# Attention with a feed-forward layer: identity made on chip, first pair transposed ahead of the bias table product, one AV in two parts, alpha early, two feed-forward tiles first

## Chip, cores, metric

One core of one Trainium2 chip. The metric is the device time of one execution in microseconds (us). The kernel before takes 390.5 us (median of three runs, 390.46 to 390.96). Each execution also comes with the span from first to last instruction (about 1.7 us shorter than the time) and with the mean granted clock of the tensor engine. All moments below are us from the start of the span. PE is the tensor engine, ACT the scalar, DVE the vector engine, POOL is GpSimd.

## The reference

```python
# q, k, v: 8 x 8 x 576 x 64; bias_table: 32 x 8; w_in: 512 x 2048; w_out: 2048 x 512; alpha: 2048
scores = np.matmul(q, k.transpose(0, 1, 3, 2)) / np.sqrt(D)
scores = scores + bias.transpose(2, 0, 1)[None]      # bias depends on |i - j| alone
attn = softmax(scores)                               # ... max, exp, sum written out
attn_out = np.matmul(attn, v)
x = attn_out.transpose(0, 2, 1, 3).reshape(4608, 512)
h = x @ w_in
g = h + np.sin(alpha * h) ** 2 / (alpha + 1e-9)
return (g @ w_out).astype(np.float32)
```

## The kernel before

The kernel emits a start-up by hand and leaves the rest to a small list scheduler, which is part of the kernel's own Python: each task has a priority, an earliest planned moment (`nb`), buffers and dependencies, and the scheduler emits tasks in the order in which its model of the engines would start them. So a moved number moves the instruction order on every engine. Names: `natb`, `nat1` are q and k as loaded; `turn`/`plan_tr` transposes them on PE with the identity `id_sb`; `u` is exp(scores), multiplied on DVE by exp(bias) (`m2r`, `mhr`), made on chip from a table product; AV multiplies `u` by `v`, whose extra column of ones gives the sum; `am`, `ca`, `cb` are single PSUM banks, `sc` are the large ones. Heads go in pairs, four pairs per batch.

```python
T_START = 7.0
T_PAIR = ((7.0, 8.5), (10.5, 13.0), (10.5, 13.0))   # earliest transposes of pairs 1 to 3
T_W = 30.0
T_WO = (56.0, 59.0, 62.0, 65.0)                     # earliest use of the quarters of w_out
WARM0 = 6
WARM1 = 1
# ... start-up
    nc.sync.dma_start(out=id_sb, in_=idm.ap())      # identity from memory
    # ... loads of q, k, v
    nc.vector.tensor_tensor(out=tabN, in0=tabN, in1=tabL, op=ALU.subtract)
    nc.scalar.activation(out=tabE, in_=tabN, func=AF.Exp)
    warm(WARM0)
    eps_ = bank("moE")                              # bias table product, bank cb
    nc.tensor.matmul(out=eps_[0:H, 0:EW], lhsT=tabE, rhs=phi_sb, start=True, stop=True)
    warm(WARM1)
    nc.scalar.activation(out=e_sb, in_=eps_[0:H, 0:EW], func=AF.Copy)
    nc.scalar.dma_start(out=e_dram.ap(), in_=e_sb)
    cast0(0, nc.vector)
    cast0(1, P_)
    # ... POOL: bias rows, V casts, w_in loads, loads of the next batches
    stage_kq(2)
    load_w_out16()                                  # w_out in four quarters
    # ... plan_tr: transposes of pair 0 are tasks like any other
# ... plan_alpha
        m = plan.add({"PE": 0.1}, mm, [], 5000, nb=20.0, new=[b])
        return plan.add({"DVE": 0.4}, cp, [m], 5000, use=[b])
# ... plan_av: per 128 rows one matmul with vh and eight with v, all after every part of u
        for i, qc in enumerate(QC[w]):
            # ... 1 + 2 * 4 matmuls
            prev = [plan.add({"PE": 0.31}, mm, us + prev, base + AV_PRI + i, ...)]
# ... plan_moe_in: first feed-forward block; three quarters of each sum can start early
            if b == 0 and f < 4:
                m = plan.add({"PE": 3 * t_pe(512)}, lambda e, mm=mm: mm(e, range(3)), xs012,
                             pri - 100, nb=T_W, after=qk_last[:], new=[hb])
                m = plan.add({"PE": t_pe(512)}, lambda e, mm=mm: mm(e, range(3, 4)), xs + [m],
                             pri, use=[hb])
```

The softmax here doesn't subtract the row's maximum and nothing guards it: scores larger than these inputs give would overflow.

## Time and profile before

| stage of the kernel before | from - to | length | what fills it |
|---|---|---|---|
| start-up | 0 - 10.30 | 10.30 | loads, bias table, first transposes |
| 24 exponentials of batch 0 | 10.30 - 32.86 | 22.56 | ACT, with gaps |
| handover to the feed-forward block | 32.86 - 38.38 | 5.52 | DVE, PE, ACT in turn |
| first block of sines | 38.38 - 54.96 | 16.58 | ACT |
| exponentials of batches 1 and 2 | 54.96 - 95.72 | 40.76 | ACT, then PE |
| the rest | 95.72 - 388.7 | 293.0 | PE |

The borders are marks: first exponential, end of the last exponential of batch 0, first sine, second load of ACT's tables ("table load 2"; the load for the sines is the one before), and table load 3 at 95.72. Of the page, the first part (busy time, share of the span, instructions) and the fourth (the chain that ended last, by engine) of the kernel before:

```profile
PE 374.4 (96%) x3381; PEld 186.8 (48%) x3381; DVE 264.7 (68%) x588; ACT 319.1 (82%) x449; POOL 82.5 (21%) x96
PE 90%; ACT 5%; DVE 1%; issue 1%; DMA 1%; ACTq 0%; DVEq 0%
```

PE has something in flight for 96% of the time, so what a change of the first 55 us can win is the moment at which PE becomes dense. One thing to know about this page: its row of tenths for the clock shows 9 from the first slice on, while the matmul spacing of the warm-ups (0.426 us for 512 columns, 0.215 later) says that the array runs at half rate until its recorded release, at 22.43. That stretch the row does not show.

### The profile page before, as it was taken

The page shows a single profiled execution, that of the slowest core. Times are in us where ns is not written, and L with a number is a line of the kernel's source. Part 1 is how long each engine was busy: PE and PEld are TensorE (multiplying, and loading weights), DVE is VectorE, ACT ScalarE, POOL GpSimd, SP SyncE. Part 2 cuts the span into 40 slices and gives each one's busy share as a digit, 9 for nine tenths or more (in the row PEclk, how much of TensorE's full clock was granted, in tenths as well). Part 3 has the DMA queues.
Part 4 walks back from the last instruction along what each step waited for, and adds up shares of the span by engine and source line. Part 5 has one row for each costly group of instructions (what it writes and reads, how often), then busy time and mean ns, then how long its engine had stood idle before and what let it go on. Part 6 is the DMA issues. An engine that isn't in the chain of part 4 may idle for free.

```text
span 388.7 us, 8498 instructions
## 1 busy us (share of the span) xinstructions
PE 374.4 (96%) x3381; PEld 186.8 (48%) x3381; DVE 264.7 (68%) x588; ACT 319.1 (82%) x449; POOL 82.5 (21%) x96
## 2 busy tenths in 40 slices
PE   5999989999999999999999999999999999999995
PEld 2466434465545544555355435643554444444442
DVE  3776976776886798669767977697669628439100
ACT  2876999999999999999999999999999629539211
POOL 5673935072530081006200400000000000000000
PEclk9999999999999999999999999999999999999999
DMA  9999999999999999969991928210120020020112
GB/s 173 205 201 218 169 186 168 153 163 140 146 162 145 179 138 139 167 90 86 153 160 47 74 31 211 64 27 29 33 68 18 29 81 1 29 81 2 65 70 81
DMA packets 151207, 42.58 MB, mean 110 GB/s; under 512 B 140344, under 2 KB 145552, under 8 KB 151168
## 3 DMA queue, kind: packets, MB, share of 16 engines
q0 software_dynamic: 89872, 19.04, 59.5%
q1 hardware_dynamic: 61072, 22.95, 32.7%
q8 instruction: 26, 0.43, 0.5%
q14 instruction: 13, 0.11, 0.1%
q10 hardware_dynamic: 224, 0.05, 0.1%
HBM read 37.76 MB, written 16.52 MB: 140 GB/s over the span
## 4 chain that ended last, share of the span: by engine, by line
PE 90%; ACT 5%; DVE 1%; issue 1%; DMA 1%; ACTq 0%; DVEq 0%
PE sc L451 43%; PE am L451 37%; PE ca L451 4%; ACT u L719 4%; PE cb L451 4%; DMA tabL<-in_bias_table_dram 1%; PE cb L560 1%; PE am L560 1%; DVE kT L540 0%; ACT L953 0%; ACT outs L538 0%; ACT sq L886 0%; DVE xp L799 0%; DVE tabN L505 0%; ACT s L879 0%
## 5 line engine op out<-in xcount | busy, mean ns | idle before, releaser
L719 ACT ACTIVATE u<-sc 128x1024 f16<-128x1024 f32 (+1 forms) x192 | 155.7, 896 | 9.0 <-PE sc L451 7.0
L451 PE MATMUL sc<-xT,w_in 128*128 128x512 f16 x576 | 133.0, 379 | 0.2 <-DVE g L893 0.2
L893 DVE SCALAR_TENSOR_TENSOR g<-sq,inv_a,sc 128x512 f16<-128x512 f16 x144 | 103.8, 746 | 25.9 <-PE am L451 21.4
L451 PE MATMUL am<-w_out,g 128*128 128x512 f16 x448 | 117.3, 382 | 0.7 <-ACT outs L538 0.7
L879 ACT ACTIVATE s<-sc,alphaT 128x512 f16<-128x512 f32 x144 | 92.5, 679 | 7.0 <-PE sc L451 6.2
L744 DVE TENSOR_TENSOR u<-u,m2r 128x512 f16<-128x512 f16 (+2 forms) x160 | 67.8, 440 | 29.2 <-ACT u L719 27.0
L451 PEld LDWEIGHTS <-g 128*128 128x128 f16 x576 | 53.6, 98 | 67.4 <-issue 14.7
L451 PEld LDWEIGHTS <-w_in 128*128 128x128 f16 x576 | 54.6, 98 | 62.8 <-issue 0.3
L451 PEld LDWEIGHTS <-u 128*128 128x128 f16 x1440 | 55.9, 98 | 17.1 <-issue 4.5
L451 PE MATMUL am<-v,u 128*128 128x65 f16 x1216 | 53.4, 194 | 0.0
L451 PE MATMUL sc<-qT,kT 64*128 64x64 f16 (+1 forms) x512 | 48.2, 296 | 2.8 <-ACT u L719 1.0
L886 ACT ACTIVATE sq<-s 128x512 f16<-128x512 f16 x75 | 46.6, 630 | 2.3 <-DVE g L893 0.5
L397 POOL DMA_DIRECT2D v<-in_v_dram x24 | 21.2, 897 | 108.3 <-PE am L451 107.1
L451 PE MATMUL am<-vh,u 128*128 128x130 f16 x152 | 33.8, 222 | 0.7 <-DVE xp L799 0.6
L888 DVE TENSOR_TENSOR sq<-s 128x512 f16<-128x512 f16 x69 | 28.9, 420 | 6.6 <-ACT s L879 6.3
L799 DVE TENSOR_TENSOR xp<-am,rd 128x384 f16<-128x384 f32 (+1 forms) x56 | 27.5, 491 | 2.3 <-DVE rd L798 0.3
L451 PEld LDWEIGHTS <-kT 64*128 64x128 f16 x512 | 13.8, 96 | 30.1 <-issue 26.8
L798 DVE RECIPROCAL rd<-am 128x6 f32<-128x6 f32 (+1 forms) x60 | 11.3, 188 | 19.4 <-PE am L451 19.0
L538 ACT ACTIVATE outs<-am 128x512 f32<-128x512 f32 x7 | 4.2, 597 | 18.5 <-PE am L451 18.5
L953 ACT ACT_TABLE_LOAD x13 | 16.7, 1283 | 0.2
L540 DVE COPY outs<-am 128x512 f32<-128x512 f32 x21 | 14.4, 687 | 3.6 <-PE am L451 3.0
L378 POOL DMA_DIRECT2D staged_q<-in_q_dram x6 | 14.4, 2396 | 7.4 <-DMA staged_q<-in_q_dram 5.4
(87 smaller groups left out, 169.0 us busy)
## 6 DMA issues: line engine op xcount, KB each, us to landing
out_dram<-outs SPq DMA_DIRECT2D x36, 256.0 KB, 2.0
staged_k<-in_k_dram POOLq DMA_DIRECT2D x6, 576.0 KB, 15.9
staged_q<-in_q_dram POOLq DMA_DIRECT2D x6, 576.0 KB, 19.9
v<-in_v_dram POOLq DMA_DIRECT2D x24, 128.0 KB, 9.3
w_in<-in_moe_w_in_dram POOLq DMA_DIRECT2D x4, 512.0 KB, 8.1
w_out<-in_moe_w_out_dram POOLq DMA_DIRECT2D x4, 512.0 KB, 18.1
xT<-xp SPq DMA_TRANSPOSE x72, 4.4
w_out<-in_v_dram SPq DMA_DIRECT2D x4, 256.0 KB, 8.5
```

What stands on the lines that cost most here:

```text
L378: nc.gpsimd.dma_start(out=dst.ap()[t].rearrange("s (h d) -> s h d", h=H), in_=src[t].rearrange("h s d -> s h d"),)
L397: nc.gpsimd.dma_start(out=vs[t % 2][:, c, :, 0:D], in_=vp[128 * c : 128 * c + 128],)
L451: nc.tensor.matmul(out=out, lhsT=lhsT, rhs=rhs, start=start, stop=stop)
L540: k_of(e).tensor_copy(out=o, in_=i)
L719: nc.scalar.activation(out=o, in_=x, func=AF.Exp, scale=0.125)
L744: nc.vector.tensor_tensor(out=io, in0=io, in1=m2[:, 2 * p : 2 * p + 2, x0 : x0 + hi - lo], op=ALU.mult,)
L799: nc.vector.tensor_tensor(out=y.rearrange("p c (z d) -> p c z d", z=2), in0=a[:, :, :, 0:D], in1=r.unsqueeze(3).to_broadcast([128, nq, 2, ...
L879: nc.scalar.activation(out=s16.v, in_=h.v, func=AF.Sin, scale=alphaT[:, f : f + 1])
L886: nc.scalar.activation(out=sq.v, in_=s16.v, func=AF.Square)
L888: k_of(e).tensor_tensor(out=sq.v, in0=s16.v, in1=s16.v, op=ALU.mult)
L893: nc.vector.scalar_tensor_tensor(out=gcell[b].v[:, f, :], in0=sq.v, scalar=inv_a[:, f : f + 1], in1=h.v, op0=ALU.mult, op1=ALU.add,)
L953: nc.scalar.preload_act_table_set(name)
```

## The change

Its intent is a shorter start: no load of the identity; transposes of the first pair before the bias table product instead of behind it; the last pair's AV of the first batch in two parts, so that most of it need not wait for the last multiplications; alpha's transpose and reciprocal moved from the handover to the beginning. With it come new planned moments, a new priority for two of the first four feed-forward tiles, and a shorter list of dependencies for one AV task of each pair in the first batch (not shown below). Cut to its core:

```diff
-T_PAIR = ((7.0, 8.5), (10.5, 13.0), (10.5, 13.0))
+T_FREE = {"PE": 7.0, "ACT": 7.5, "DVE": 7.85}
+T_QT0 = 7.85
+T_PAIR = ((6.6, 7.3), (10.5, 13.0), (10.5, 13.0))
-WARM1 = 1
-    nc.sync.dma_start(out=id_sb, in_=idm.ap())
+    P_.memset(id_sb, 1.0)
+    P_.affine_select(out=id_sb, in_=id_sb, pattern=[[-1, 128]], compare_op=ALU.is_equal,
+                     fill=0.0, base=0, channel_multiplier=1)
+    cast0(0, nc.vector)
+    cast0(1, P_)
+    def turn0(kq):  # six transposes into one bank, copy by DVE
+        ...
+    turn0(0)
-    eps_ = bank("moE")
+    eps_ = new_ps("am0")
     nc.tensor.matmul(out=eps_[0:H, 0:EW], lhsT=tabE, rhs=phi_sb, start=True, stop=True)
-    warm(WARM1)
     nc.scalar.activation(out=e_sb, in_=eps_[0:H, 0:EW], func=AF.Copy)
     nc.scalar.dma_start(out=e_dram.ap(), in_=e_sb)
-    cast0(0, nc.vector)
-    cast0(1, P_)
+    turn0(1)
 # plan_alpha
-        m = plan.add({"PE": 0.1}, mm, [], 5000, nb=20.0, new=[b])
-        return plan.add({"DVE": 0.4}, cp, [m], 5000, use=[b])
+        m = plan.add({"PE": 0.1}, mm, [], -50, nb=8.0, new=[b])
+        return plan.add({"DVE": 0.4}, cp, [m], -50, use=[b])
 # plan_av
+        split = t == 0 and p == NP - 1 and w == 0
+        if split:
+            def part(e):  # the 18 matmuls on the first three parts of u
+                ...
+            prev = [plan.add({"PE": 0.62}, part, us[:3], base + AV_PRI, nb=T_V[t], new=[ab], use=[ub])]
 # plan_moe_in
-                             pri - 100, nb=T_W, after=qk_last[:], new=[hb])
+                             pri - (100 if f < 2 else 1), nb=T_W, after=qk_last[:], new=[hb])
```

More of the change, by code (lines that the diff above doesn't have):

```diff
@@ L109, in run @@
     def run(self, t0):
-        free = {e: t0 for e in ("PE", "ACT", "DVE", "POOL", "DMA", "SP")}
+        free = {e: T_FREE.get(e, t0) for e in ("PE", "ACT", "DVE", "POOL", "DMA", "SP")}
         todo = list(self.tasks)
@@ L254 @@
     phi_h = nc.inline_tensor(phi_np, "phi_const")
-    idm = nc.inline_tensor(np.eye(128, dtype=np.float16), "ident")
     idf = nc.inline_tensor(np.eye(NF, dtype=np.float32), "identf")
@@ L493 @@
         load_nat(nat1[:, kq, 0:2], 2, 4, src[0], P_)
+    P_.memset(id_sb, 1.0)
+    P_.affine_select(
+        out=id_sb, in_=id_sb, pattern=[[-1, 128]], compare_op=ALU.is_equal, fill=0.0, base=0,
+        channel_multiplier=1,
+    )
     vp = v[0].rearrange("h s d -> s h d")
@@ L507 @@
     warm(WARM0)
-    eps_ = bank("moE")
+    cast0(0, nc.vector)
+    cast0(1, P_)
+    def turn0(kq):
+        c = bank("moE").bitcast(F16)
+        for i in range(SI):
+            nc.tensor.transpose(
+                out=c[:, i * SN : i * SN + SN], in_=natb[:, kq, i], identity=id_sb[0:SN, 0:SN]
+            )
+        nc.vector.tensor_copy(
+            out=(qTs if kq else kTs)[0][:, 0, :].rearrange("d (p i) -> d p i", i=SI),
+            in_=c[:, 0:S].rearrange("d (i p) -> d p i", i=SI),
+        )
+    turn0(0)
+    eps_ = new_ps("am0")
     nc.tensor.matmul(out=eps_[0:H, 0:EW], lhsT=tabE, rhs=phi_sb, start=True, stop=True)
-    warm(WARM1)
     nc.scalar.activation(out=e_sb, in_=eps_[0:H, 0:EW], func=AF.Copy)
     nc.scalar.dma_start(out=e_dram.ap(), in_=e_sb)
-    cast0(0, nc.vector)
-    cast0(1, P_)
+    turn0(1)
     clear(P_, 1)
@@ L547, in plan_tr, with tail @@
         far = kq == 0 and (t == 1 or p > FAR)
+        def tail(e):
+            for z in range(2):
+                r = slice(64 * z, 64 * z + 64)
+                nc.vector.tensor_copy(
+                    out=kts[t][r, p, r], in_=kTs[t][r, p, 512:S]
+                )
+        if t == 0 and p == 0:
+            x = Task({}, None, [], 0)
+            x.end = T_QT0
+            return [x], [x] if kq else [plan.add({"DVE": 0.25}, tail, [x], pri + 30)]
         def mm(e):
@@ L552, in mm @@
                 x = i * SN
-                if t == 0 and p == 0:
-                    nc.tensor.transpose(
-                        out=c.v[:, x : x + SN], in_=natb[:, kq, i], identity=id_sb[0:SN, 0:SN]
-                    )
-                    continue
                 for z in range(2):
@@ L570, in cp @@
             copy_on(e, dst.rearrange("d (p i) -> d p i", i=SI), pin)
-        m = plan.add({"PE": 0.4 if t == 0 and p == 0 else 0.5}, mm, deps, pri, nb, new=[b])
+        m = plan.add({"PE": 0.5}, mm, deps, pri, nb, new=[b])
         eng = {"DVE": 0.75, "ACT": 0.72}
         if t == 0:
-            eng = {"ACT": 0.72} if p == 0 and kq else {"DVE": eng["DVE"]}
+            eng = {"DVE": eng["DVE"]}
         x = plan.add(eng, cp, [m], pri, use=[b])
@@ L593, in plan_tr @@
             return [x], []
-        def tail(e):
-            for z in range(2):
-                r = slice(64 * z, 64 * z + 64)
-                nc.vector.tensor_copy(
-                    out=kts[t][r, p, r], in_=kTs[t][r, p, 512:S]
-                )
         return [x], [plan.add({"DVE": 0.25}, tail, [x], pri + 30)]
@@ L770, in plan_av @@
         prev = []
+        split = t == 0 and p == NP - 1 and w == 0
+        if split:
+            def part(e):
+                av.v = bank(ab.tag)
+                for i, qc in enumerate(QC[w]):
+                    for z in range(2):
+                        for c in range(3):
+                            x0 = 2 * VC * i + VC * z
+                            full(av.v[:, x0 : x0 + VC], u.v[:, 4 * z + c, qc : qc + 128],
+                                 vs[t % 2][:, c, 2 * p + z, :], (i, z, c) == (0, 0, 0), False)
+            prev = [plan.add({"PE": 0.62}, part, us[:3], base + AV_PRI, nb=T_V[t], new=[ab],
+                             use=[ub])]
         for i, qc in enumerate(QC[w]):
             def mm(e, i=i, qc=qc):
-                if i == 0:
+                if i == 0 and not split:
                     av.v = bank(ab.tag)
@@ L777, in mm @@
                 full(av.v[:, x0 : x0 + 2 * VC], u.v[:, 8, qc : qc + 128], vhs[t % 2][:, p, :],
-                     True, False)
+                     not split, False)
                 for z in range(2):
-                    for c in range(4):
+                    for c in range(3 if split else 0, 4):
                         full(av.v[:, x0 + VC * z : x0 + VC * z + VC],
                              u.v[:, 4 * z + c, qc : qc + 128], vs[t % 2][:, c, 2 * p + z, :],
-                             False, z == 1 and c == 3)
-            prev = [plan.add({"PE": 0.31}, mm, us + prev, base + AV_PRI + i,
-                             nb=T_V[t] if t < 2 else 0.0, new=[ab] if i == 0 else [],
-                             use=[ub] if i == 0 else [ub, ab])]
+                             False, z == 1 and c == 3 and (not split or i == nq - 1))
+            needs = us
+            if t == 0 and w == 1 and i == 0:
+                needs = [done[(0, c)] for c in range(4)] + [done[(1, 4)]]
+            prev = [plan.add({"PE": 0.12 if split else 0.31}, mm, needs + prev,
+                             base + AV_PRI + i, nb=T_V[t] if t < 2 else 0.0,
+                             new=[ab] if i == 0 and not split else [],
+                             use=[ub] if i == 0 and not split else [ub, ab])]
             avs.setdefault(t, []).extend(prev)
```

## The prediction

> **What bounds the kernel now.** I read the page first: PE is busy for 96% of the span and 90% of the chain that ended last. So the span is PE work plus whatever keeps PE from it, and I asked next where PE is not dense. The table of busy time by stage (each row: stretch and length in us, then busy us with instruction counts of PE, weight loads, DVE, ACT, POOL, then clock, DMA share, GB/s) answers that:
>
> ```profile
> 0.00:10.30 10.30, 6.25 (x36) 2.61 (x36) 4.40 (x14) 2.73 (x4) 5.74 (x16) 1.00 0.97 178
> 10.30:22.40 12.10, 11.84 (x125) 6.15 (x123) 8.08 (x16) 10.20 (x12) 9.49 (x15) 1.00 1.00 199
> 22.40:32.87 10.47, 9.37 (x160) 6.57 (x158) 9.46 (x32) 9.61 (x12) 5.35 (x8) 1.00 1.10 203
> 32.87:38.38 5.51, 5.09 (x67) 3.31 (x67) 2.74 (x10) 2.11 (x4) 2.61 (x2) 1.00 1.24 227
> 38.38:54.96 16.58, 14.67 (x149) 7.13 (x148) 15.40 (x27) 16.25 (x28) 11.95 (x15) 1.00 1.79 176
> 107.00:145.00 38.00, 38.00 (x370) 19.09 (x369) 30.52 (x69) 36.25 (x51) 11.06 (x10) 1.00 1.64 155
> ```
>
> From about 65 us PE is full (38.00 of 38.00 in the last row), and the instruction order of the two builds differs only up to the middle of the second batch; after that 540 runs of equal PE instructions follow one another. The change can therefore only move the moment at which the dense part begins. Before that the bound is another: 10.30 to 32.87 is the chain of 24 exponentials on ACT (22.57 us, of which the gaps below are 2.43), 32.87 to 38.38 is the handover to the first feed-forward block, and 38.38 to 54.96 is ACT again, 16.25 of 16.58 us busy.
>
> The timeline (start, length, engine, line, what, count, idle before it and its releaser) shows the joints:
>
> ```profile
> 6.91 0.59 ACT L511 ACTIVATE e_sb<-cb 8x512 f16<-8x512 f32 x1 [0.67 <-PE cb L509]
> 7.54 0.64 PE L554 MATMUL cb<-id_sb,natx 96*128 96x96 f16 x6
> 10.30 4.80 ACT L719 ACTIVATE u<-sc 128x1024 f16<-128x1024 f32 x5 [0.95 <-PE sc L451]
> ...
> 21.34 0.60 ACT L719 ACTIVATE u<-sc 128x512 f16<-128x512 f32 x1 [0.65 <-PE sc L451]
> ...
> 22.87 4.80 ACT L719 ACTIVATE u<-sc 128x1024 f16<-128x1024 f32 x6 [0.94 <-DMA w_in<-in_moe_w_in_dram]
> ...
> 28.05 4.80 ACT L719 ACTIVATE u<-sc 128x1024 f16<-128x1024 f32 x6 [0.38 <-PE sc L451]
> ...
> 33.19 0.35 DVE L540 COPY xT<-am 128x384 f16<-128x384 f16 x1
> ...
> 33.59 0.22 PE L451 MATMUL am<-vh,u 128*128 128x130 f16 x1
> ...
> 36.66 2.32 PE L451 MATMUL sc<-xT,w_in 128*128 128x512 f16 x10
> ...
> 38.38 1.84 ACT L879 ACTIVATE s<-sc,alphaT 128x512 f16<-128x512 f32 x3 [1.18 <-PE sc L451]
> ```
>
> The first pair's transposes start at 7.54, 0.04 us after ACT has read bank cb (6.91 + 0.59): they wait for the bank of the bias product, not for the identity, whose weight loads are already let through at 6.81. The gaps before the exponentials are 0.46 (at 15.56), 0.65, 0.94 and 0.38. The last AV starts 0.05 us after DVE has emptied bank am (33.19 + 0.35 = 33.54). Ten matmuls in a row stand ahead of and around what the first sine waits for.
>
> [...] the six warm-up matmuls take 2.74 us, spacing (2.74 - 0.61)/5 = 0.426; the twelve at 40.90 take 2.75, spacing (2.75 - 0.38)/11 = 0.215. The change from slow to fast falls near 22.5 us, so the whole start-up runs at half rate though the page prints a clock of 9 tenths. [...] Here the 8 KB write of the bias row, issued at 7.52, released POOL at 12.85, with all engines busy. [...] The 32x8 subtraction took 0.78 us beside POOL's 0.82 us cast, while a 128x16 operation takes 0.17 elsewhere. [...]
>
> **The change part by part.**
>
> *Identity on chip.* It removes one 32 KB load, issued at 1.69 and landing 4.2 us later (5.9), before the cast of k ends at 6.63. Worth nothing directly. It adds a memset and a select on POOL ahead of two DMA issues. Estimate, from 0.31 us for a 260-wide memset and 0.60 for a 512-wide cast: 0.5 to 0.7 us together. POOL idles 1.11 us before its cast at 5.16, so this is hidden. A side effect: the first V load on that queue no longer waits for an earlier load (it was issued at 3.33), so V moves up some 1.6 us and competes earlier.
>
> *Pair 0 ahead of the bias product.* k's transposes can start after the cast, 6.63 + 0.17 = 6.80 instead of 7.54; k's copy then runs 7.48 to 8.24. The bias product follows at 7.25, its copy on ACT ends near 8.46, and the bias row goes out about 0.95 us later than 7.52. q's transposes run 7.70 to 8.38. Their copy is now DVE's, 8.42 to 9.17 (0.75), where ACT ended at 9.35. But all 24 transposes of pair 1 now stand before the first QK, and the second dozen needs the bank that this copy empties: 9.22 + 12 x 0.052 = 9.84, so QK at 9.84 instead of 9.65, and the first exponential near 10.5 instead of 10.30. **Plus 0.2.**
>
> *Order of QK and AV.* The first AV now stands behind QK of the third pair's first block instead of before the second pair's last. That removes the 0.65 and 0.94 gaps, whose cause is AV waiting in order for V casts (POOL, 20.21) and bias products (DVE, 20.44). In their place 27 AV matmuls sit in one piece, 1.8 us at the slow spacing (18 took 1.2 us at 21.23), against one 0.96 us exponential in hand: a gap of 0.9 to 1.4 and a smaller one after it. A warm-up matmul plus transposes early in pair 0 costs some 0.3, the gap at 15.56 stays near 0.5, the late ones near 0.4. Sum 2.3 to 2.7 for 2.43. **Zero to plus 0.3.** The later bias row and V casts end before AV wants them (near 21.4), so they cost nothing.
>
> *AV in two parts.* The 18 early matmuls need bank am, which is free at 33.54 whichever way they are grouped, and they already follow 0.05 us later. The third multiplication ends at 33.87, about when its matmul comes up. **0 to minus 0.15.**
>
> *Alpha early.* It takes 0.17 + 0.17 + 0.25 = 0.59 us from DVE at 30.3 to 30.9, between multiplications with slack; PE sets that stretch. **0 to minus 0.1.**
>
> *Order of the first feed-forward matmuls.* In the row of ten, the one that finishes the first block was seventh (after two partial blocks of three) and is now fourth. Three matmuls less are 3 x 0.215 = **minus 0.65** for the first sine (37.73): its other input, ACT's copy at 36.86 + 0.33 = 37.19, is there in time.
>
> *The stage after it.* It is full on ACT. The scheduler hands it nine squares instead of eight (one more at 0.63) and DVE one fewer. **Plus 0.3 to 0.6.**
>
> Sum: +0.2 + 0.15 - 0.1 - 0.05 - 0.65 + 0.45 = 0.0. It all passes into the dense part nearly one for one.
>
> **The rivals.** *First: the starts gain what they were ordered for.* If the late V and bias row turn out earlier because loads start sooner, and the clock is released before the first AV (27 matmuls then take 0.9 us instead of 1.8), the gaps shrink from 2.43 to about 1.2: 389.0 us. For it: the constants look fitted to measured starts. Against: QK still stands behind pair 1. *Second: the clock comes later.* AV, the densest work, begins a microsecond later, and if the release follows it, the second AV group is slow too, 0.6 us more: 391.2. [...] *Fourth: DMA contention.* V half a load earlier delays the bias table row or pair 1's loads (landing 6.1 and 6.7, wanted 8.3 and 9.2); over 1.5 us of delay would show, and each us costs one.
>
> **Range and chances.** My sum says no change. Somebody who placed these starts by hand presumably saw a gain, and the first rival is the one with that weight; I move 0.6 us towards it: 389.9. The four open terms are each about half a microsecond, which gives 388.8 to 391.0. Two per cent is 7.8 us, more than all gaps named here together, so nearly all the chance lies within it.
>
> **What would show it.** Right: k's transposes near 6.8; first exponential at 10.3 to 10.6; gaps before 33 us adding to 2.0 to 2.7, the largest right after the first AV; the last AV starting just after the copy that empties am; first sine 5.0 or less after the last exponential instead of 5.5; a stage of sines 0.3 to 0.6 longer; then equal lengths from 65 us on. Wrong: a first exponential before 10.0 (then the reorder pays and I misread the bank wait), a gap sum under 1.5, a select over 1 us, or spacing that turns fast well away from 22.5 us.

The sum comes to 0.0, that is 390.5 us, and the move of 0.6 us towards the first rival makes the 389.9.

## The result, and the profile after

390.71 us (median of four runs, 390.65 to 390.86) against 390.67 before on the same occasion: ratio 1.0001, 95% interval 0.9984 to 1.0018, the same. All ratios here are the mean time of one kernel's fast runs over that of the other's of the same rounds, so not quite the ratio of the medians quoted.

The page of the changed kernel, parts one and four:

```profile
PE 374.5 (96%) x3382; PEld 186.4 (48%) x3382; DVE 264.7 (68%) x587; ACT 319.4 (82%) x450; POOL 82.9 (21%) x98
PE 86%; ACT 6%; DVE 3%; issue 2%; DMA 1%; ACTq 0%; DVEq 0%
```

The busy times are equal within 0.4 us. What differs is where the time lies. The table by stage of the changed kernel (columns as in the prediction):

```profile
10.77:32.49 21.72, 20.06 (x270) 11.36 (x268) 16.18 (x45) 19.97 (x24) 14.56 (x21) 1.00 0.97 193
32.49:37.70 5.21, 4.99 (x68) 3.20 (x67) 2.88 (x11) 2.44 (x5) 2.49 (x2) 1.00 1.31 219
37.70:54.65 16.95, 16.14 (x154) 7.51 (x153) 15.71 (x26) 16.78 (x29) 12.27 (x16) 1.00 1.76 185
107.00:145.00 38.00, 38.00 (x371) 19.08 (x370) 30.57 (x68) 36.29 (x50) 11.08 (x10) 1.00 1.66 153
```

Read against the kernel before: the start is 0.47 longer (10.77 against 10.30), the exponentials 0.84 shorter (21.72 against 22.56), the handover 0.31 shorter (5.21 against 5.52), the sines 0.37 longer (16.95 against 16.58). Sum at table load 2: -0.31 us (54.65 against 54.96). At table load 3 it is +0.15 (95.87 against 95.72), and +0.15 it stays to the last load (287.89 against 287.74). So 0.46 us were lost between 55 and 96 us, in a part whose instructions the change does not touch.

The timeline of the changed kernel at its start (start, length, engine, line, what, count, idle before and releaser):

```profile
2.76 0.24 POOL L493 MEMSET id_sb<- 128x128 f16 x1
3.09 0.29 POOL L494 TENSOR_SCALAR_AFFINE_SELECT id_sb<-id_sb 128x128 f16<-128x128 f16 x1
6.88 0.66 PE L518 MATMUL cb<-id_sb,natx 96*128 96x96 f16 x6 [2.88 <-DVE natx L459]
9.50 0.69 PE L584 MATMUL am<-id_sb,u 96*64 96x96 f16 x12 [0.23 <-DVE qT L521]
10.77 2.85 ACT L735 ACTIVATE u<-sc 128x1024 f16<-128x1024 f32 x3 [2.09 <-PE sc L451]
...
16.90 5.98 ACT L735 ACTIVATE u<-sc 128x1024 f16<-128x1024 f32 x7 [0.56 <-PE sc L451]
23.19 5.01 ACT L735 ACTIVATE u<-sc 128x1024 f16<-128x1024 f32 x6 [0.31 <-PE sc L451]
28.50 4.00 ACT L735 ACTIVATE u<-sc 128x1024 f16<-128x1024 f32 x5 [0.30 <-PE sc L451]
```

The identity is made in 0.53 us and is ready 3.5 us before its first use. The first transposes start at 6.88 instead of 7.54. But the first exponential is later: twelve transposes of the second pair (9.50, released by the copy of q) still stand before the first scores. All gaps among the 24 exponentials add to 1.75 us, against 2.75 before (counted here over all 24; the prediction counted 2.43).

The handover, changed kernel:

```profile
30.50 1.49 DVE L760 TENSOR_TENSOR u<-u,m2r 128x128 f16<-128x128 f16 x4
31.91 0.19 DVE L832 RECIPROCAL rd<-am 128x6 f32<-128x6 f32 x1
...
33.16 0.35 DVE L557 COPY xT<-am 128x384 f16<-128x384 f16 x1
33.56 0.71 PE L451 MATMUL am<-v,u 128*128 128x65 f16 x18
...
36.64 2.32 PE L451 MATMUL sc<-xT,w_in 128*128 128x512 f16 x10
37.70 1.84 ACT L913 ACTIVATE s<-sc,alphaT 128x512 f16<-128x512 f32 x3 [0.53 <-PE sc L451]
```

Here lies the first surprise. The exponentials end 0.37 us earlier than before (32.49 against 32.86), but the last AV starts at 33.56 against 33.59. It waits for bank am, which DVE empties at 33.16 + 0.35 = 33.51, and DVE gets there no earlier: it works without a break from 30.50 through four multiplications to the reciprocal at 31.91. In the kernel before, the same stretch of DVE was alpha's three operations (30.29 to 30.94) and then

```profile
30.86 0.96 DVE L744 TENSOR_TENSOR u<-u,m2r 128x768 f16<-128x768 f16 x2
31.74 0.19 DVE L798 RECIPROCAL rd<-am 128x6 f32<-128x6 f32 x1
```

What the exponentials had gained in this trace was given back to DVE. From the end of that copy, 33.51, to the first sine, 37.70, are 4.19 us; before, 4.84.

The second surprise is the loss after 55 us. The timeline of the changed kernel around the first AV of the second batch:

```profile
60.40 0.64 PE L451 MATMUL am<-v,u 128*128 128x65 f16 x8
62.74 3.46 ACT L735 ACTIVATE u<-sc 128x1024 f16<-128x1024 f32 x5 [0.65 <-PE sc L451]
```

and of the kernel before:

```profile
56.26 12.99 ACT L719 ACTIVATE u<-sc 128x1024 f16<-128x1024 f32 x16
60.71 0.41 PE L451 MATMUL am<-v,u 128*128 128x65 f16 x8
```

Eight matmuls take 0.64 us instead of 0.41, and the exponential behind them waits 0.65 us, where before sixteen ran without a gap. The table of busy time in steps of one microsecond shows why, in its column of the clock (the third from the end); the changed kernel:

```profile
59.00:60.00 1.00, 1.00 (x5) 0.23 (x4) 0.64 (x2) 1.00 (x2) 0.14 (x1) 0.50 1.22 196
60.00:61.00 1.00, 1.00 (x13) 0.69 (x12) 0.43 (x2) 1.00 (x2) 0.00 (x0) 0.50 1.21 196
61.00:62.00 1.00, 1.00 (x20) 0.88 (x18) 0.02 (x1) 1.00 (x2) 0.00 (x0) 0.71 1.21 195
```

and the kernel before:

```profile
59.00:60.00 1.00, 1.00 (x3) 0.15 (x1) 0.56 (x1) 1.00 (x3) 0.06 (x1) 0.51 1.22 197
60.00:61.00 1.00, 1.00 (x15) 0.47 (x15) 0.68 (x2) 1.00 (x3) 0.00 (x0) 1.00 1.21 196
```

Both traces have one stretch of 3.41 us at half rate in this place, and no other between the first release and the last microseconds: 56.56 to 59.97 before, 58.16 to 61.57 after. Before, it ends ahead of AV; after, it lies on it. This gave the theory: **the change wins a few tenths at the handover, and a half-rate stretch on the first AV of the second batch takes them back.** The rivals: the dense part is bound by PE's own work and returns any lead; or another wait stands there; or the place of the stretch is an accident of the run.

### The profile page after: what moved, and what is told of

Same layout as the page of the kernel before. It is cut to its first block, busy times and chain, and to the rows that moved or that the text cites. A ratio compares the mean times of both kernels' runs of the same rounds, so it can differ in the third digit from the quotient of the medians.

```text
span 388.9 us, 8502 instructions
## 1 busy us (share of the span) xinstructions
PE 374.5 (96%) x3382; PEld 186.4 (48%) x3382; DVE 264.7 (68%) x587; ACT 319.4 (82%) x450; POOL 82.9 (21%) x98
## 3 DMA queue, kind: packets, MB, share of 16 engines
HBM read 37.73 MB, written 16.52 MB: 139 GB/s over the span
## 4 chain that ended last, share of the span: by engine, by line
PE 86%; ACT 6%; DVE 3%; issue 2%; DMA 1%; ACTq 0%; DVEq 0%
PE sc L451 40%; PE am L451 37%; ACT u L735 4%; PE ca L451 4%; PE cb L451 4%; ACT s L913 1%; DMA tabL<-in_bias_table_dram 1%; DVE g L927 1%; ACT sq L920 1%; DVE xn L833 1%; DVE u L760 0%; DVE qT L557 0%; PE am L584 0%; PE cb L584 0%; ACT outs L555 0%
## 5 line engine op out<-in xcount | busy, mean ns | idle before, releaser
L920 ACT ACTIVATE sq<-s 128x512 f16<-128x512 f16 x76 | 47.4, 631 | 2.3 <-DVE g L927 0.5
L451 PE MATMUL am<-vh,u 128*128 128x130 f16 x152 | 33.6, 222 | 0.5 <-DVE xp L833 0.3
L987 ACT ACT_TABLE_LOAD x13 | 16.7, 1283 | 0.2
```

What stands on the lines that cost most here:

```text
L451: nc.tensor.matmul(out=out, lhsT=lhsT, rhs=rhs, start=start, stop=stop)
L920: nc.scalar.activation(out=sq.v, in_=s16.v, func=AF.Square)
L987: nc.scalar.preload_act_table_set(name)
```

## The experiments

Twelve runs were made, all correct. The profile of each is one execution, and executions of one kernel differ by 1 us and more (the kernel before took 389.22 to 390.70, 389.44 to 391.48 and 389.43 to 392.41 us in the three jobs beside the experiments), so small effects are read from lengths between marks of one trace, and whole times only from five rounds. How well a length repeats differs: with the same instruction order the handover came to 5.20 to 5.21 in five traces, the stage of sines within 0.12 in five traces of the changed kernel and its neighbours but only within 0.25 in two of the kernel before (16.58, 16.83), and the first exponential only within 0.6 us. "Offset" is a variant's mark minus that of the first profile of the kernel before.

### The changed kernel again, and with the clock kept up

No edit for the first. For the second, ten idle matmuls (on zeros, into a bank that is not in use) between the scores of the second batch's first pair; the instruction order is otherwise the same. The same with eight in the kernel before.

```diff
                     sc.v = new_sc(order[seq.index((p, i)) % nreg], 2)
+                    n_w = {1: 1, 2: 4, 3: 5}.get(i, 0) if t == 1 and p == 0 else 0
+                    if n_w:                       # kernel before: {1: 4, 3: 4}
+                        x_w = new_ps("am1")
+                        for _ in range(n_w):
+                            full(x_w, zz[:, 0:128], zz, True, True)
```

> The changed kernel once more, unchanged, to see what stays the same from run to run. In its first profile the second batch's table load began 0.31 us ahead of the kernel before (54.65 against 54.96), but from 67 us on it ran 0.15 us behind; between them the record of the array clock shows half rate from 58.16 to 61.57, in the kernel before from 56.56 to 59.97. Theory A (the half-rate stretch ate the gain): the stretch is 3.41 us long again and starts within one such length of 58; where it covers the 27 AV matmuls near 60.4 (1.6 us instead of 0.95) the exponential near 62 waits 0.6 us; time 390.7. Theory C (the position of the stretch is an accident of the run, the two kernels differ by nothing): the stretch lands elsewhere in this run and the order of the two kernels' times turns round by up to 0.5 us.

> Ten idle 128x512 matmuls on zeros put where PE waits between the first QK blocks of the second batch; nothing else moves. Theory A (half-rate clock ate the gain): no half-rate record between 54 and 66 us, the 27 AV matmuls near 60.3 take 0.95 us, no gap over 0.2 us before the eighth exponential of that batch, third table load near 95.2 instead of 95.87, time 390.0 to 390.2 (0.5 to 0.7 less than after). Theory B (the order of QK, AV and output matmuls in the second batch ate it): full rate, but the exponential near 62 still waits 0.4 us or more and the time stays within 0.15 us of 390.7.

> The same in the kernel before (four idle matmuls in each of two waits of PE in the second batch). Theory A: its half-rate stretch (56.56 to 59.97) lay on QK blocks for which ACT did not wait, so removing it gives 0 to 0.2 us; the distance to after_warm is then 0.4 to 0.7 us, the lead that the change has at 55 us. Theory B: no change at all here and the distance between the two stays near zero.

Measured, five rounds on one chip: the changed kernel again 391.38 us (390.82 to 391.73), ratio to the kernel before 1.0023 (1.0005 to 1.0041); with the clock kept up 390.42 us (389.26 to 390.85), ratio 0.9995 (0.9975 to 1.0014); the kernel before with the clock kept up 390.36 us (389.9 to 391.38), ratio 1.0000 (0.9982 to 1.0019); the kernel before itself 390.27 us (389.44 to 391.48).

In the trace of the repeat, two half-rate stretches lie together, 55.23 to 62.06, and the gap behind AV is 0.96 us. With the idle matmuls no half-rate stretch is left after the first release (mean clock of that execution 0.999; in the repeat 0.974), the gap is 0.09 us, and the eighth exponential of the batch stands 7.54 us after table load 2 (8.76 in the repeat, 8.09 in the first profile). So the clock made that gap. But the time expected from this, 390.0 to 390.2 us, and a distance of 0.4 to 0.7 us to the kernel before with the same care, did not come: the lead is lost all the same. The changed kernel with the clock kept up, from table load 2 on:

```profile
55.54 10.64 ACT L740 ACTIVATE u<-sc 128x1024 f16<-128x1024 f32 x13
66.11 0.38 PE L451 MATMUL am<-w_out,g 128*128 128x512 f16 x1 [0.73 <-DMA w_out<-in_moe_w_out_dram]
66.85 2.48 ACT L740 ACTIVATE u<-sc 128x1024 f16<-128x1024 f32 x3 [0.67 <-PE sc L451]
```

Thirteen exponentials in a row; then PE comes to the first matmul on the last quarter of the output weights and waits 0.73 us for it to land, and the next exponential waits 0.67 us. The offset goes from -0.51 before this wait to +0.08 after it and at table load 3. The weights are queued on POOL behind loads of the third batch (issues at 43.18, landing 12.8 to 20.6 us later).

### Those two loads exchanged

```diff
-    stage_kq(2)
     load_w_out16()
+    stage_kq(2)
```

> The same exchange in before_warm, whose wait at that place was only 0.3 us. Theory D: it gains 0.2 to 0.5 us over before_warm, so that after_warm_wout is ahead of it by 0.2 to 0.5 us, the lead of the change at the second batch's table load (0.31 to 0.35 in the profiles). Theory E: the two stay level within 0.2 us.

> after_warm, in which the output weights are loaded ahead of the k and q of the third batch (two groups of DMA issues on POOL exchanged). In after_warm the clock stayed at full rate and the exponential near 62 came 0.96 us earlier than in after, but at 66.1 PE waited 0.73 us for the last quarter of the output weights and the lead was gone. Theory D (the landing of the output weights near 65 to 66 us is a wall that no earlier lead passes): with the exchange that quarter lands before 58, no wait for it, and the lead stays: third table load at 94.8 to 95.2, time 389.5 to 390.0, that is 0.5 to 0.9 less than after_warm on the same chip. Theory E (PE work alone decides from 62 us on): no wait, but the gap reappears elsewhere and the time stays within 0.2 us of after_warm.

Measured: slower by 0.6 to 0.8%. The kernel before so changed 392.05 us, ratio 1.0059 (1.0035 to 1.0083). Its waits between 50 and 100 us:

```profile
PE sc L451 <- DMA qT<-staged_q: 1.4, 1, 1.4
```

Now the third batch's q is late by 1.4 us, and the offset goes from +1.32 to +2.75 at this place. (The +1.39 at table load 2 is older: this trace has a half-rate stretch at 25.98 to 29.39, among the first batch's exponentials, whose gaps add to 4.11 us.) The changed kernel so changed took 391.97 to 398.22 us in five runs, two of which (397.93, 398.22) count as slow, so that the ratio of 1.008 (1.0046 to 1.0114) rests on three; a sixth, the one with the profile, took 543.57 us at a mean granted clock of 0.666. That run is slow and nothing about the kernel is read from it. In the kernel before, the exchange only moved the wait from one transfer to another: the 512 KB quarters of the output weights took 16.7 to 18.1 us from issue to landing in ten traces with the old order (median of each trace), 10.8 issued ahead (three of the four).

### The last quarter used later

```diff
-T_WO = (56.0, 59.0, 62.0, 65.0)
+T_WO = (56.0, 59.0, 62.0, 67.5)
```

once in the changed kernel with the clock kept up, once in the kernel before with the clock kept up and with the one line of the change that gives two of the first four feed-forward tiles priority.

> after_warm (clock kept full through the second batch's first AV) with the matmuls on the last quarter of the output weights planned 2.5 us later. Theory (the lead of the changed kernel was first spent on half-rate AV matmuls and then, once these are mended, on the wait for the last quarter of the output weights, 0.73 us at 66.11): with both taken away no gap over 0.3 us among the second batch's sixteen exponentials, the third sine table load at 95.0 to 95.5 us (95.80 in after_warm, 95.72 in the kernel before), and a time 0.3 to 0.7 us under the kernel before of the same rounds, ratio 0.9982 to 0.9992. Rival (the dense part is bound by the tensor engine's own sum of work, so that a lead at its start is always returned): the gaps go but the load stays at 95.6 to 95.9 and the ratio at 0.9995 to 1.0005. Second rival (another wait stands behind the weights, as with the swapped loads): a new gap over 0.5 us behind a transfer.

> The kernel before with three edits of which only one is in the change: the first two ff tiles of the last pair put early (worth 0.65 us at the handover), the clock kept full, and the last quarter of the output weights planned 2.5 us later. It lacks the chip-made identity, the early p1 transposes, the split AV and the early alpha. Theory: handover 4.9 us (5.52 before), stage near 16.9, table load 2 at 54.0 to 54.5, third table load at 95.0 to 95.5, and time 0.3 to 0.7 us under the kernel before. If after_warm_late is faster than this by over 0.2 us the remaining parts (start, split, alpha) are worth something; if the two are equal within 0.2 they are worth nothing. Rival (lead always returned): third load 95.5 to 95.8, ratio 0.9995 to 1.0005.

Measured, five rounds: 390.67 us (390.47 to 391.53), ratio 1.0009 (0.9988 to 1.0030), and 390.74 us (389.81 to 392.34), ratio 1.0015 (0.9990 to 1.0040), beside 390.27 of the kernel before. Neither is faster. My expectation of 0.3 to 0.7 us less fell in both.

In the trace of the first, both earlier gaps are gone, and the offset is still -0.50 at the twenty-second exponential of the batch. Then, further on:

```profile
78.48 0.81 PE L451 MATMUL am<-w_out,g 128*128 128x512 f16 x3
...
80.28 4.32 ACT L740 ACTIVATE u<-sc 128x1024 f16<-128x1024 f32 x5 [0.48 <-PE sc L451]
```

Output matmuls that had been put off stand in a place where there was none before, ahead of the scores of the next exponential, which waits 0.48 us. The offset is +0.25 at table load 3. No transfer is named: this fits the rival of a PE that is full, so that what is put off has to be paid later. In the trace of the second the lead did survive: offset -0.92 at table load 2, -0.70 at table load 3 and -0.71 at the last. That execution took 389.81; the other five of the same kernel, at mean clocks of 0.982 to 0.999, took 390.53 to 392.34. So 0.7 us in one trace are no gain in the time, as long as the executions of one kernel scatter more than that.

### The priority of two feed-forward tiles, taken out and put in alone

```diff
-                             pri - (100 if f < 2 else 1), nb=T_W, after=qk_last[:], new=[hb])
+                             pri - 100, nb=T_W, after=qk_last[:], new=[hb])
```

in the changed kernel, and the reverse in the kernel before; one look each.

> The changed kernel with the old order of the first feed-forward matmuls. The prediction's step: the finishing matmul of the first block is fourth instead of seventh in a row of ten, worth 3 x 0.215 = 0.65 us for the first sine, and the stage that follows then has one square more on ACT, 0.3 to 0.6 us. So here: first sine 5.8 to 5.9 us after the last exponential (5.21 in the changed kernel's three profiles), and a stage from first sine to table load of 16.4 to 16.7 instead of 16.92 to 17.04. If the handover stays at 5.2 the order of these matmuls was not what gained.

> The kernel before with only the new order of these matmuls. By the same step: first sine 4.85 to 4.95 us after the last exponential instead of 5.52, and a stage of 16.9 to 17.1 instead of 16.58 to 16.83, so a table load about 0.3 us earlier relative to the last exponential. If the handover shrinks by less than 0.4, something else (the copies of the last pair) sets it.

Measured: without it 390.35 us, handover 5.86 us (5.21 with it), stage of sines 16.58 us (16.95 with it). Put alone into the kernel before: 389.99 us, handover 4.88 us (5.52 without), stage 16.93 us (16.58 without). The line is worth -0.65 us in the handover, the same in both kernels. The +0.36 in the stage after it is less sure: the kernel before with the clock kept up has 16.83 without the line, so the difference lies between 0.1 and 0.4 us. From the last exponential to table load 2 the line leaves 0.2 to 0.5 us: 22.13 to 22.25 with it and 22.44 without in the changed kernel, 21.81 and 21.91 with it against 22.10 and 22.36 in the kernel before. It is the only part of the change whose effect shows there. In the second of these traces PE waits for the output weights again, 1.3 us in two places (54.86 and 58.20), but the offset is still -0.87 well behind them. It falls to -0.49 at another wait, for the third batch's q:

```profile
74.92 0.61 PE L451 MATMUL sc<-qT,kT 64*128 64x512 f16 x4 [0.32 <-DMA qT<-staged_q]
```

The kernel before with the clock kept up loses 0.22 us of its lead in the same place, so a third thing can take a lead back.

### The second transposes of pair 1 behind the first scores

```diff
-T_PAIR = ((6.6, 7.3), (10.5, 13.0), (10.5, 13.0))
+T_PAIR = ((6.6, 8.0), (10.5, 13.0), (10.5, 13.0))
```

> In the changed kernel the q transposes of pair 1 go behind the first QK instead of ahead of it (one planned start, 7.3 to 8.0). The prediction's step: pair 1's second dozen of transposes, which waits for the bank that the copy of q empties, costs the first exponential 0.6 us. If so the first exponential comes at 10.15 to 10.3 instead of 10.77. Whether it reaches the end: with the later gaps on ACT unchanged the last exponential of the first batch ends 0.3 to 0.5 earlier than 32.51 and the time falls to 390.2 to 390.5; if PE fails to feed ACT later (transposes now interrupt QK), gaps grow by as much and the time stays at 390.7.

Measured, five rounds: 390.99 us (390.36 to 391.65), ratio 1.0017 (0.9996 to 1.0037). The first exponential starts at 10.07 (10.77 and 10.20 in the two profiles of the changed kernel). These moments scatter with the landing of the loads (9.62 to 10.77 over the seven traces with the new start), so the clean reading is the distance from the start of q's copy to the first exponential: 1.46 us, against 2.08 in all seven. The transposes do cost 0.62 us there. But the gaps among the 24 grow from 1.75 and 1.85 to 2.64 us, and the copy that empties am ends at 33.85, later than in every other trace of the table below. What the start gains, the chain of exponentials loses. Not all of that loss is the edit's: in this trace the clock was released only at 22.93 (20.61 in the changed kernel), so two of the three parts of the first AV, which begins at 21.77, ran at half rate (0.64 us for eight matmuls, 0.41 in the third). Besides, 45 AV matmuls stand before the next scores where 27 did, and the gap there is 1.13 us (0.31). The run doesn't separate the two.

### AV in one part, and alpha late

```diff
-        split = t == 0 and p == NP - 1 and w == 0
+        split = False
```

```diff
-        m = plan.add({"PE": 0.1}, mm, [], -50, nb=8.0, new=[b])
-        return plan.add({"DVE": 0.4}, cp, [m], -50, use=[b])
+        m = plan.add({"PE": 0.1}, mm, [], 5000, nb=20.0, new=[b])
+        return plan.add({"DVE": 0.4}, cp, [m], 5000, use=[b])
```

each alone in the changed kernel, one look each.

> The changed kernel with the last pair's AV of the first batch accumulated in one part again. The prediction gave the split 0 to -0.15 us: the handover from the last exponential to the first sine then stays at 5.2 to 5.4 us (5.21 with the split), since the exponential-side half of AV is at most four of the eighteen matmuls. Rival (the split is what brought the handover from 5.52 to 5.21): handover 5.5 or more. The order of the ff row moves a little with it, which can shift the stage by 0.1 to 0.3 us; time 390.3 to 391.3, within the scatter of one look.

> The changed kernel with alpha computed at its old late place. The prediction gave the early alpha 0 to -0.1 us because nothing waits for it until the first sine: gaps among the first batch's exponentials 1.7 to 2.0 us, handover 5.1 to 5.3, stage 16.8 to 17.1, table load 2 within 0.3 us of the changed kernel's 54.65 after the start is allowed for. Rival (alpha's operations in the first batch hold the vector engine while it is on the path at the handover): handover 0.2 us or more longer with the late alpha.

Measured: 390.52 and 391.33 us, and in both the handover is 6.05 us. By the numbers this is the rivals' side twice; by the traces it is neither's cause. In both, the scheduler has put three feed-forward matmuls ahead of the last AV. With alpha late:

```profile
33.62 1.10 PE L451 MATMUL sc<-xT,w_in 128*128 128x512 f16 x3
...
34.56 0.71 PE L451 MATMUL am<-v,u 128*128 128x65 f16 x18
```

The third of them waits for ACT's copy (33.96 to 34.29; with AV in one part the profile names this wait, 0.17 us), and AV stands behind it. Measured to the mark before that order matters, the end of the copy that empties am, the distance from the last exponential is 1.01 us in the changed kernel, 1.01 with AV in one part, 1.06 with alpha late. So neither part is worth more than 0.05 us up to there, and what they are worth after it can't be told apart from the order which the scheduler makes of them.

These two traces also settle the clock question from another side. Neither has idle matmuls, and neither happens to have a half-rate stretch after the first release. With AV in one part:

```profile
56.16 13.12 ACT L735 ACTIVATE u<-sc 128x1024 f16<-128x1024 f32 x16
...
60.59 0.41 PE L451 MATMUL am<-v,u 128*128 128x65 f16 x8
```

Sixteen exponentials in a row, no gap over 0.09 us, and the eighth 7.54 us after table load 2 (7.53 with alpha late). The change's own instructions do not make the gap of 0.65 us.

### All marks together

| kernel | copy out of am ends | from there to first sine | stage of sines | eighth exponential after table load 2 | half rate on its AV | offset at table load 2, at 3 |
|---|---|---|---|---|---|---|
| before | 33.54 | 4.84 | 16.58 | 7.40 | no | 0, 0 |
| before, clock kept up | 32.91 | 4.85 | 16.83 | 7.32 | no | -0.37, -0.14 |
| before, priority | 32.84 | 4.19 | 16.93 | 7.53 | no | -1.00, -0.49 |
| before, priority, clock, late quarter | 32.82 | 4.18 | 17.04 | 7.53 | no | -0.92, -0.70 |
| after | 33.51 | 4.19 | 16.95 | 8.09 | yes | -0.31, +0.15 |
| after, again | 33.03 | 4.20 | 17.04 | 8.76 | yes, longer | -0.69, +0.44 |
| after, clock kept up | 33.12 | 4.20 | 16.92 | 7.54 | no | -0.72, +0.08 |
| after, clock, late quarter | 33.60 | 4.20 | 16.92 | 7.53 | no | -0.24, +0.25 |
| after, transposes later | 33.85 | 4.20 | 16.93 | 7.74 | no, ends 0.4 ahead | +0.02, +0.16 |
| after, no priority | 32.74 | 4.85 | 16.58 | 8.05 | yes | -0.79, -0.15 |
| after, AV in one part | 32.71 | 5.04 | 17.11 | 7.54 | no | -0.10, +0.02 |
| after, alpha late | 33.71 | 4.99 | 16.97 | 7.53 | no | +0.71, +0.84 |

The first column answers what the new start is worth. The four kernels with the old start empty am at 32.8 to 33.5, mean 33.03; the seven with the new one (without the run of later transposes) at 32.7 to 33.6, mean 33.20. Three traces with the same start-up order (the changed kernel, its repeat, and with the clock kept up) already differ by 0.48. The new start gains nothing that can be seen.

Between marks the account is steadier (the same traces of the table). From the start of q's copy to the first exponential it is 1.60 us with the old start (1.79 in one trace) and 2.08 with the new one. The gaps among the 24 exponentials add to 2.12 to 2.75 us with the old start and to 1.75 to 2.00 with the new one. From the last exponential to the end of the copy that empties am it is 0.68 us with the old start and 1.01 to 1.06 with the new one, also with AV in one part or alpha late, so neither of these makes the difference alone. About half a microsecond won in the gaps is paid back at both ends.

## Why the prediction was right, and where it was not

Right: no change, and the time inside the range: 390.71. The plain sum, 0.0 us, was nearer than the 389.9; the 0.6 us that I moved towards a hoped-for gain was the only part of the number without a row behind it. That the sum came out is in part luck, since its terms erred in both directions. In the first profile the start cost 0.47 (0.2 predicted), the exponentials took 0.84 less (0.15 more predicted), the handover shrank by 0.31 (0.8 predicted with AV and alpha), the stage of sines grew by 0.37 (0.45 predicted), and then 0.46 was lost where nothing had been predicted.

*Identity on chip, worth nothing.* Shown: 0.24 and 0.29 us on POOL, in idle time, ready 3.5 us ahead of use.

*Pair 0 ahead of the bias product, plus 0.2.* Right where it can be read between marks. Transposes at 6.88 (6.80 predicted), first exponential at 10.77 (10.5 predicted). That pair 1's transposes hold the scores is shown by the run with them later, by 0.62 us between marks. Set against the old start they cost 0.48 (2.08 against 1.60 from the start of q's copy). The total of plus 0.2 is not shown: traces with this start-up order begin at 9.62 to 10.77, those with the old one at 9.75 to 10.51.

*Order of QK and AV, zero to plus 0.3.* Wrong. Gaps add to 1.75, 1.85 and 1.87 us in the three traces, under the 2.0 given as the lowest; the gap after the first AV is 0.31, not 0.9 to 1.4. The failed step is "1.8 us at the slow spacing": the clock was released at 20.61, ahead of the first AV at 21.75, so its 27 matmuls took 1.0 us. The first rival named exactly this. The same holds for the 0.94 us gap of the kernel before, which I put down to AV's waits: it is 0.43 in three other traces with that order, released at 20.58, 19.15 and 13.37, so about half of it goes with the slow clock. The moment of release differs from run to run: in the kernel with the transposes later it came at 22.93, and the same 27 matmuls took 1.4 us. But the first rival's 389.0 did not follow, because the 0.84 us that the exponentials saved went into the later start (0.47) and the wait for DVE (0.34).

*AV in two parts, 0 to minus 0.15; alpha early, 0 to minus 0.1.* Up to the copy out of am 0.01 and 0.04, as sized. "The 18 early matmuls need bank am" was the right reason. Beyond that mark it stays open, as each edit reorders the feed-forward matmuls.

*Order of the first feed-forward matmuls, minus 0.65.* Right to the hundredth in two kernels, and the first sine, predicted at 37.73, was at 37.70. But the handover of "5.0 or less" was 5.21: the last exponential ends 0.37 earlier than before while the copy that frees am does not.

*The stage after it, plus 0.3 to 0.6.* The size was right, +0.37, and +0.35 with the one line alone in the kernel before (less beside the 16.83 of its other trace). The reason is not borne out. I gave it to one more square on ACT, nine in the stage instead of eight; but with AV in one part and with alpha late the stage has eight squares and still takes 17.11 and 16.97 us. What lengthens it stays open.

*"It all passes into the dense part nearly one for one."* This failed. -0.31 us at 54.65 became +0.15 at 95.87. I had seen a clock of 0.83 in a row and not asked which instructions lie there, and I had read "from about 65 us PE is full" off a row that begins at 107. In the kernel before, PE has work for 8.87 of the 10 us from 55 on and 9.72 of the next 10, and is full from 75 only; in that part the waits lie. What is shown: the half-rate stretch on the first AV makes the gap behind it (0.61 to 0.96 us in the three traces where the stretch lies on AV, and at most 0.09 us in the nine where it does not); with it gone, the wait for the output weights took the lead in one trace, deferred output matmuls in another, and the third batch's q a part of it in a third. That the loss is a law of the dense part is not shown, since in the kernel before with three edits 0.70 of 0.92 us survived.

*The range.* Too narrow in its reasons though not in its result: the repeat in another job had a median of 391.38, outside it; in its trace two half-rate stretches lay on the AV.

One thing stays open. By mean clock, 13 of the 33 executions of the kernel before that ran beside the experiments had 0.998 or more, so no late stretch (one of 3.41 us takes 0.004 off the mean, which was 0.996 in the first profile of the changed kernel), and two more had 0.982, as the trace with AV in one part, whose only half rate lies before 22 us and in the last microseconds. None of the ten of the changed kernel had either (0.974, or 0.991 to 0.996). On one chip the four such executions of the kernel before had spans of 387.4, 387.4, 387.9 and 387.9 us, and its six at 0.993 to 0.994 had 388.3 to 388.9; on another chip the two kinds overlap. If the change makes the stretch more likely, this may be why the repeat was 0.2% slower. But neighbours of the changed kernel (AV in one part, alpha late) ran without it, and three traces decide nothing about a chance. Where the half rate came can be read in the two first traces: the fall is 34.13 us after the release in the kernel before (22.43 to 56.56) and 37.55 us in the changed one (20.61 to 58.16), 10 and 11 times the 3.41 us of the stretch itself. Counted in such steps from the release to 100 us, the step before the fall had 1.83 us of PE work in the kernel before and 1.53 in the changed one, all others at full rate 2.57 or more. In the repeat the 3.43 us before its fall had 1.92. But with AV in one part and with alpha late, 3.41 us with as little work (1.44 us in 53.50 to 56.91, and 1.48 in 54.50 to 57.91) brought no fall, so little work alone does not do it. That it depends on where such steps happen to lie over the light stretch around 55 us, an accident of the run as the last rival had it, is my reading; no run tested it. With the clock kept up in both kernels, 390.42 and 390.36 us, the change is worth nothing either way. No version beat the kernel before.

## What to carry to other kernels

Follow a lead to the next engine before you count it: here the gaps among the exponentials shrank by half a microsecond and nothing used it, because the start came later and the bank that mattered was freed by DVE, which was full (no break from 30.50 us to the reciprocal at 31.91). Where a stage of light PE work comes just before dense work, look at the clock column in steps of a microsecond, since here a half-rate stretch on the first AV of the dense part left gaps of 0.61 to 0.96 us, more than the tenths one is after. And repeat a profile before explaining tenths: three traces of the same start-up order differed by half a microsecond, as much as the whole change.
